# Hand-placed buffers in one memory tile, late weights over attention buffers, and a mixture token part spread over head pairs

## The chip, the core and the metric

The kernel runs on one core of a Trainium2 chip. A core has five engines that run side by side and meet at semaphores: TensorE (PE in the profile, with PEld for its weight loads), VectorE (DVE), ScalarE (ACT), GpSimd (POOL) and SyncE (SP). Matrix products go to a small memory of eight banks, PSUM; everything else is worked on in the larger SBUF; DMA engines carry data between the chip's main memory and SBUF. The metric is device time in microseconds, the median of the runs shown, lower being better.

## The reference

Attention comes first, then a soft mixture of experts over its result. There are 8 batches, 12 heads, 448 tokens and a head width of 64. The mixture sees the 3584 tokens with 768 features each, and has 8 experts with 4 slots each and a hidden width of 1024.

```
scores = (q @ k^T) / sqrt(64);  m = max over keys;  e = exp(scores - m)
attn   = e / (sum(e) + exp(-m) + 1e-9);   x = (attn @ v) as [3584 tokens, 768]
logits = x @ phi                                  # [3584, 32 slots]
d = softmax of logits over the tokens;  slot_input = d^T @ x
slot_out[e] = relu(slot_input[e] @ w1[e]) @ w2[e] # eight experts, four slots each
c = softmax of logits over the slots;   out = c @ slot_out
```

All inputs are 32-bit floats. The kernel works on 16-bit floats (bf16), which its transfers write directly. The eight experts' weights are 50 MB in main memory; the kernel handles them as 32 pieces of 768 KB in bf16 (expert, matrix, half). Queries, keys and values together are 33 MB in main memory.

## The kernel before, in words

**A fast path and a fallback.** The kernel holds two complete programs. The fast path leaves out the maximum m, since exp(scores) without it divides to the same result as long as no sum overflows. It keeps every denominator in `den_all`, and at its end it counts on how many of the 112 partitions all denominators are below a limit: `fine` compares (L495), `good` takes the minimum per partition (L496), and a matrix product of `good` with a column of ones gives the count, which is cast to a whole number in `n_good` (L498, L499). Each engine then loads that number and branches (L593, L594): if it is below 112, the whole of `general_path` (L23 to L172) runs behind the fast path and computes everything again, with maxima, one head at a time and 112 query rows at a time.

**`general_path`.** Its attention is 8 x 12 x 4 = 384 blocks of 112 query rows. Each block makes one score product (L56), a maximum on DVE (L58) and its scaling (L59), an exponential with its sum on ACT (L62), a second exponential of the maximum (L64), two sums and a reciprocal on DVE (L65 to L67), four transposes of the exponentials on PE (L70), their copy on DVE (L72), four products with the values (L75) and a division on DVE (L77). Per head there are two more copies (L52). The transposes and the output have one PSUM buffer each, the scores two. Behind it come 32 blocks of token logits (L88 to L97), a softmax over all tokens, 32 blocks of slot inputs (L106 to L112), the experts one after the other with one buffer for each weight matrix (L124 to L148), and 32 blocks of output with one output buffer (L151 to L172). A scheduler sets its instructions' order, under a queue per engine.

**The fast path's attention.** It is written under a manual schedule: each engine's queue is in the order of the text. The 96 heads are taken as 48 pairs, six to a batch; the loop of L468 runs over pairs `g`, and inside it over four parts `c`. In one round the pair `g` gets its scores (`scores`, L319) and its exponentials on ACT (L321), the pair `g-1` is multiplied with its values and divided (`attend`, L332 to L342), and the pair `g+1` is transposed (`transposes`, L309, copied by DVE at L314). POOL copies the pair `g+2` out of the staging buffers (`arrange`, L299 to L301) and also issues all loads (`load_in`, L250; `load_weight`, L229). The values have four buffers `va`, the exponentials two. A wait in POOL's queue therefore holds up every load behind it.

**The mixture's token part.** `moe_pieces(b-1)` is a list of nine pieces for a finished batch: three transposes of its tokens (L357, L360), two halves of the logits (L373) with the running softmax over tokens, transposes of the softmax weights, two slot-input products (L430), and a transpose of the slot softmax. One piece is run in each of the last two parts of a round, from the second pair of the next batch on.

**Weights and tail.** Staging takes six buffers of the size of a weight piece, two sets of three, each holding a whole batch. Weight pieces go to seventeen buffers of their own; three are issued with each batch. After the last round six pieces go to the staging buffers, and the remaining nine to a new pool, `late`, whose memory was that of the attention (L510 to L513). The experts run in two rounds of four (L536 to L570); each round needs both matrices of its four experts. The output is formed in eight pieces of 1344 KB (L578 to L591).

Of the kernel before, what the change touches and what calls it, by code (L numbers as in the profile page):

```python
# [19 lines left out]
DEN_LIMIT = float(2.0 ** 60)  # L20
# [155 lines left out]
def kernel(  # L176
# [23 lines left out]
    NG = B * HP  # L200
    scale = 1.0 / (D ** 0.5)
    SP_ = 464
    ND = DD // 2

    cst = ctx.enter_context(tc.tile_pool(name="cst", bufs=1))

    with ExitStack() as fast:
        fast.enter_context(tc.manual_schedule())


        units = fast.enter_context(tc.tile_pool(name="units", bufs=1))
        UW = H * T * D

        def unit(i, shape, name):
            u = units.tile([128, UW], BF16, tag=f"u{i}", name=name)
            return u

        NU = 23
        free_units = list(range(6, NU))
        wt = {}  # L220

        def load_weight(e, m, half, u):
            if m == 0:
                dst = u.rearrange("p (j f) -> p j f", j=KC)
                src = moe_w1[e].rearrange("(j p) f -> p j f", p=128)[:, :, ts(half, F // 2)]
            else:
                dst = u.rearrange("p (k d) -> p k d", d=DD)
                src = moe_w2[e].rearrange("(k p) d -> p k d", p=128)[:, ts(half, FK // 2), :]
            nc.gpsimd.dma_start(out=dst, in_=src)  # L229
            wt[e, m, half] = dst  # L230

        weight_order = [(e, m, h) for e in range(E) for m in range(2) for h in range(2)]


        qn, kn, va = {}, {}, {}
        ident = cst.tile([128, 128], BF16, name="ident")
        acc = cst.tile([NS, DD], F32, name="acc")
        dsum = cst.tile([NS, 1], F32, name="dsum")
        ones = cst.tile([128, 1], BF16, name="ones")
        n_good = cst.tile([1, 1], I32, name="n_good")  # L240
        cT_all = cst.tile([128, B, 128], BF16, name="cT")

        heads_src = lambda a, b, h0, h1: a[b, h0:h1].rearrange("h (p t) d -> p h (t d)", t=T)

        def load_in(b, parts):
            st = [unit(3 * (b % 2) + i, None, f"in{3 * (b % 2) + i}") for i in range(3)]
            for h0, h1 in parts:
                for a, u in zip((k, q, v), st):
                    vw = u.rearrange("p (h x) -> p h x", h=H)
                    nc.gpsimd.dma_start(out=vw[:KT, h0:h1, :], in_=heads_src(a, b, h0, h1))  # L250
            kn[b], qn[b], vn[b] = [u.rearrange("p (h t d) -> p h t d", h=H, t=T) for u in st]

        vn = {}
        load_in(0, [(0, 2), (2, H)])
        make_identity(nc, ident)
        nc.vector.memset(acc, 0.0)
        nc.vector.memset(cT_all, 0.0)
        nc.vector.memset(dsum, 0.0)
        nc.vector.memset(ones, 1.0)

        with ExitStack() as at:
            ent = at.enter_context
            abuf = ent(tc.tile_pool(name="abuf", bufs=1))
            va_buf = [abuf.tile([128, 2, T, D + 1], BF16, name=f"va{i}") for i in range(4)]
            eT_buf = [abuf.tile([128, T, 2, SP_], BF16, name=f"eT{i}") for i in range(2)]
            for i in range(4):
                nc.gpsimd.memset(va_buf[i][:, :, :, D:], 1.0)
            for i in range(2):
                nc.vector.memset(eT_buf[i][:, :, :, S:], 0.0)
            phi_sb = abuf.tile([128, KC, 4, NS], BF16, name="phi")  # L270
            phi_f = abuf.tile([128, KC, NS], F32, name="phif")
            Z = abuf.tile([128, S], BF16, name="Z")
            den_all = abuf.tile([128, NG * 2 * T], F32, name="den")
            nc.sync.dma_start(out=phi_f, in_=moe_phi.rearrange("(j p) s -> p j s", p=128))
            nc.vector.memset(Z, 0.0)
            for r in range(4):
                nc.vector.tensor_copy(phi_sb[:, :, r, :], phi_f)
            p_in = ent(tc.tile_pool(name="p_in", bufs=3))
            p_qk = ent(tc.tile_pool(name="p_qk", bufs=2))
            p_x = ent(tc.tile_pool(name="p_x", bufs=2))  # L280
            p_xT = ent(tc.tile_pool(name="p_xT", bufs=1))
            p_w = ent(tc.tile_pool(name="p_w", bufs=2))
            ps_S = ent(tc.tile_pool(name="ps_S", bufs=2, space=PSUM))
            ps_t = ent(tc.tile_pool(name="ps_t", bufs=1, space=PSUM))
            ps_o = ent(tc.tile_pool(name="ps_o", bufs=2, space=PSUM))
            ps_m = ent(tc.tile_pool(name="ps_m", bufs=1, space=PSUM))

            qk, tp, xb, ob = {}, {}, {}, {}

            k2, q2, va = {}, {}, {}  # L290

            def arrange(g):

                b, hp = divmod(g, HP)
                hs_ = slice(2 * hp, 2 * hp + 2)
                k2[g] = p_in.tile([128, T, 2, D], BF16, name="k2")
                q2[g] = p_in.tile([128, T, 2, D], BF16, name="q2")
# [5 lines left out]
            def transposes(g, c):  # L303
                b, hp = divmod(g, HP)
                if c == 0:
                    tp[g] = ps_t.tile([128, 2 * S], BF16, name="tp")
# [42 lines left out]
            def moe_pieces(b):  # L349
# [18 lines left out]
                def logits(i):  # L368
                    def f():
# [5 lines left out]
                        if i == 0:  # L375
                            return
# [249 lines left out]
```

## Time and profile before

| what | value |
| --- | --- |
| median of three runs (range) | 338.07 us (337.82 to 339.64) |
| time of the profiled execution | 338.76 us |
| its span, first to last instruction | 337.0 us |
| first and last exponential of the attention (L321) | 10.07 and 236.06 us |
| late weights: first issued, last landed | 253.9 and 292.1 us |
| first product of the output (L583) | 297.34 us |
| DMA traffic | 53.3 MB moved, of which 11.0 MB is output |

The span is measured inside one profiled execution, and the time of that execution is 1.76 us longer than its span; it lies 0.2% above the median. The rows of the groups list read as: line, engine, operation, output and inputs with their shapes and count, then the busy time and mean duration of one, then the idle time of that engine just ahead of these instructions and who ended it. In the slices of the span each digit is a tenth of a slice's time.

### The profile page before, as it was taken

The numbers are of one execution on the slowest core, as the hardware profiler recorded it, in microseconds if no ns is written. First come the engines' busy times: TensorE is split into PE (matmuls) and PEld (weight loads), VectorE is DVE, ScalarE is ACT, GpSimd is POOL, SyncE is SP. The second block draws the span as 40 slices with busy tenths as digits, with TensorE's granted clock in tenths as the row PEclk, the third lists the DMA queues.
The fourth block names the chain that finished last, engine by engine and source line by source line (L and its number), as shares of the span: only waits on it lengthen the run. The fifth ranks groups of instructions, "written<-read, shape, count | busy, mean of one in ns | idle before, by whom it ended". The sixth has DMA issues, their size and how long they took to land.

```text
span 337.0 us, 7264 instructions
## 1 busy us (share of the span) xinstructions
PE 234.8 (70%) x2963; PEld 133.8 (40%) x2963; DVE 167.0 (50%) x497; ACT 194.4 (58%) x245; POOL 134.3 (40%) x223
## 2 busy tenths in 40 slices
PE   0439999799799899979989978988640565641210
PEld 0125566456456446545645645644310122310000
DVE  3104456657567656675665757667451020153440
ACT  1237898689789769879867978988020000033330
POOL 8195494294377438439427443460007300000000
PEclk9999999789999969999978999999755595775555
DMA  7999999989959949979947900069927999539994
GB/s 95 162 123 202 202 159 205 169 108 203 208 71 199 209 70 191 205 129 157 204 77 90 160 2 0 2 95 210 208 52 113 208 211 207 107 113 341 343 342 179
DMA packets 55530, 53.34 MB, mean 158 GB/s; under 512 B 1856, under 2 KB 54592, under 8 KB 54592
## 3 DMA queue, kind: packets, MB, share of 16 engines
q0 software_dynamic: 53680, 41.68, 81.2%
q1 hardware_dynamic: 1808, 11.11, 9.4%
q8 instruction: 25, 0.41, 0.5%
q14 instruction: 17, 0.14, 0.1%
HBM read 83.46 MB, written 11.01 MB: 280 GB/s over the span
## 4 chain that ended last, share of the span: by engine, by line
PE 34%; DMA 20%; ACT 20%; DVE 15%; issue 6%; POOL 2%; ACTq 0%; DVEq 0%; SPq 0%; POOLq 0%
ACT eT L321 16%; DMA late<-in_moe_w_dram 11%; PE o L332 11%; PE s L319 9%; DMA out_dram<-ot 6%; PE m L430 4%; PE m L373 3%; PE tp L309 3%; DMA in<-in_q_dram 3%; DVE xT L360 3%; DVE x L342 2%; DVE qk L314 2%; DVE ot L587 2%; ACT Z L388 2%; PE m L357 2%
## 5 line engine op out<-in xcount | busy, mean ns | idle before, releaser
L321 ACT ACTIVATE eT<-s 112x896 bf16<-112x896 f32 x192 | 166.6, 915 | 43.8 <-PE s L319 41.4
L332 PE MATMUL o<-va,eT 112*128 112x65 bf16 x1536 | 89.8, 201 | 4.9 <-ACT eT L321 4.5
L332 PEld LDWEIGHTS <-eT 112*128 112x128 bf16 x1536 | 62.9, 101 | 49.1 <-issue 41.2
L319 PE MATMUL s<-qk 64*128 64x448 bf16 x384 | 74.4, 383 | 6.8 <-ACT eT L321 5.3
L301 POOL COPY va<-in 112x512 bf16<-112x512 bf16 x48 | 29.9, 623 | 94.5 <-PE o L332 92.3
L339 DVE TENSOR_SCALAR den<-o 112x4 f32<-112x4 f32 x96 | 15.3, 159 | 60.9 <-PE o L332 59.2
L342 DVE TENSOR_TENSOR x<-o,rd 112x256 bf16<-112x256 f32 x96 | 40.7, 424 | 3.3
L309 PE MATMUL tp<-ident,k 112*128 112x112 bf16 x192 | 32.1, 223 | 13.4 <-POOL k L299 13.4
L314 DVE COPY qk<-tp 128x896 bf16<-128x896 bf16 x48 | 29.4, 612 | 11.0 <-PE tp L309 11.0
L309 PE MATMUL tp<-ident,q 112*128 112x112 bf16 x192 | 32.0, 225 | 3.2 <-POOL q L300 3.2
L319 PEld LDWEIGHTS <-qk 64*128 64x128 bf16 x384 | 20.9, 94 | 33.1 <-issue 19.3
L299 POOL COPY k<-in 112x512 bf16<-112x512 bf16 x48 | 30.0, 624 | 2.5 <-DMA in<-in_k_dram 2.5
L300 POOL COPY q<-in 112x512 bf16<-112x512 bf16 x48 | 29.9, 622 | 2.3 <-DMA in<-in_q_dram 2.3
L309 PEld LDWEIGHTS <-k 112*128 112x128 bf16 x192 | 18.2, 102 | 14.4 <-POOL k L299 14.0
L587 DVE COPY ot<-f 112x1536 f32<-112x1536 f32 x8 | 14.1, 1757 | 17.1 <-DMA out_dram<-ot 15.4
L589 ACT COPY ot<-f 112x1536 f32<-112x1536 f32 x8 | 11.5, 1438 | 18.9 <-DMA out_dram<-ot 17.7
L583 PE MATMUL f<-sor,cT 32*128 32x384 bf16 x64 | 6.7, 470 | 21.2 <-ACT ot L589 20.3
L309 PEld LDWEIGHTS <-q 112*128 112x128 bf16 x192 | 19.6, 102 | 3.7 <-POOL q L300 3.7
L430 PE MATMUL m<-x,dz 112*128 112x384 bf16 x64 | 18.1, 422 | 1.8 <-DVE acc L436 1.1
L229 POOL DMA_DIRECT2D late<-in_moe_w_dram x9 | 7.2, 833 | 30.1 <-DVE rs L524 28.2
L341 DVE RECIPROCAL rd<-den 112x4 f32<-112x4 f32 x96 | 17.1, 178 | 3.3
L229 POOL DMA_DIRECT2D in<-in_moe_w_dram x23 | 18.3, 819 | 0.0
(80 smaller groups left out, 205.6 us busy)
## 6 DMA issues: line engine op xcount, KB each, us to landing
in<-in_moe_w_dram POOLq DMA_DIRECT2D x23, 768.0 KB, 18.5
out_dram<-ot SPq DMA_DIRECT2D x8, 1344.0 KB, 6.1
late<-in_moe_w_dram POOLq DMA_DIRECT2D x9, 768.0 KB, 19.9
in<-in_k_dram POOLq DMA_DIRECT2D x7, 672.0 KB, 7.3
in<-in_q_dram POOLq DMA_DIRECT2D x7, 672.0 KB, 10.4
in<-in_v_dram POOLq DMA_DIRECT2D x7, 672.0 KB, 12.8
in<-in_k_dram POOLq DMA_DIRECT2D x1, 560.0 KB, 7.5
in<-in_q_dram POOLq DMA_DIRECT2D x1, 560.0 KB, 9.5
```

The source lines that it names most:

```text
L229: nc.gpsimd.dma_start(out=dst, in_=src)
L299: nc.gpsimd.tensor_copy(k2[g][:KT].rearrange("p t h d -> p h t d"), kn[b][:KT, hs_])
L300: nc.gpsimd.tensor_copy(q2[g][:KT].rearrange("p t h d -> p h t d"), qn[b][:KT, hs_])
L301: nc.gpsimd.tensor_copy(va[g][:KT, :, :, :D], vn[b][:KT, hs_])
L309: nc.tensor.transpose(tp[g][:, ds(i * S + t * KT, KT)], n[:KT, t].rearrange("p h d -> p (h d)"), ident[:KT, :KT])
L314: nc.vector.tensor_copy(qk[g], tp[g])
L319: nc.tensor.matmul(s[:, h, :S], qk[g][ds(h * D, D), ds(c * KT, 128)], qk[g][ds(h * D, D), ds(S, S)], start=True, stop=True)
L321: nc.scalar.activation(eT_buf[g % 2][:KT, c, :, :S], s[:KT, :, :S], AF.Exp, scale=scale)
L332: nc.tensor.matmul(o[:, t, :], eT_buf[g % 2][:KT, j, h, ds(t * KT, 128)], va[g][:KT, h, j, :], start=(j == 0), stop=(j == T - 1))
L342: nc.vector.tensor_mul(xb[b][:KT, :, ds((2 * hp + h) * D, D)], o[:KT, :, :D], rd[:KT].unsqueeze(2).to_broadcast([KT, T, D]))
L430: nc.tensor.matmul(m, lg[2][:KT, t, :], xb[b][:KT, t, ts(half, ND)], start=(t == 0), stop=(t == T - 1))
L587: nc.vector.tensor_copy(o[:KT, :, ts(half, ND)], f[:KT, :, :ND])
```

## The change

The fast path is written anew around one tile `mem` of 106,072 bf16 elements per partition, from which `take` hands out places one behind the other; `general_path` is as it was.

- **Weights.** The order is now all 16 pieces of the first matrix, then the 16 of the second. Piece `i` goes to `unit[i]`. Units 0 to 21 are their own; 22 to 24 also hold the staging; 25 to 31 are laid over the attention's buffers. The last two pieces are each loaded in two halves.
- **Staging.** `load_in` loads half a batch (three pairs); a stage is three places of 1536 elements.
- **Denominators.** A row of the value buffer under an extra contraction row carries 1 + 1e-9, so that the sum comes out of the product; `rd_all` holds the reciprocals, and the limit is on these. Value buffers: three.
- **Token part.** Each round transposes the tokens of pair `g-2` and adds one product to the logits; the softmax over tokens, the slot inputs and the slot softmax follow in the last parts of later rounds. Transposes of all kinds share the one PSUM buffer `ps_t`.
- **Experts.** Both rounds of four experts add up in one PSUM tile: their slots are laid into 32-column groups with zeros elsewhere. The selection product is gone.
- **Check.** `fine` is now written over `xT` and `good` over the first column of `Z`. `good` is written before the experts; the last `load_weight` is issued between the two halves of the first matrix, and the product that counts `good` stands behind both halves.
- **Output.** Sixteen pieces of 672 KB out of four buffers.

```diff
-DEN_LIMIT = float(2.0 ** 60)
+RDEN_LIMIT = float(2.0 ** -60)
...
+        mem = ent(tc.tile_pool(name="mem", bufs=1)).tile([128, 106072], BF16, name="mem")
...
+        unit = [take(UW) for _ in range(NW + 3)]
+        late = top[0]
+        xbuf0 = take(T * DD)
+        kq = [[take(T * 2 * D) for _ in range(2)] for _ in range(2)]
...
+        xbuf1 = take(T * DD)
+        va2 = take(va_w)
+        xT = take(S)
+        Z = take(S)
...
+        NL = (top[0] - late) // UW
+        unit += [mem[:, late + i * UW:late + (i + 1) * UW] for i in range(NL)]
...
+        st = [[u[:, i * 1536:(i + 1) * 1536] for u, i in s_] for s_ in
+              (((unit[NW], 0), (unit[NW], 1), (unit[NW + 1], 0)),
+               ((unit[NW + 2], 0), (unit[NW + 2], 1), (unit[NW + 1], 1)))]
...
+            if i + 2 < len(w_order):
+                nc.gpsimd.dma_start(out=dst, in_=src)
+            else:
+                for n in range(2):
+                    nc.gpsimd.dma_start(out=dst[:, ts(n, 2), :], in_=src[:, ts(n, 2), :])
...
-                    nc.vector.tensor_scalar(dn, o[:KT, :, D], 1e-9, 1.0, ALU.add, ALU.add)
-                    rd = p_w.tile([128, T], F32, name="rd")
-                    nc.vector.reciprocal(rd[:KT], dn)
+                    rd = rd_all[:KT, ds((g * 2 + h) * T, T)]
+                    nc.vector.reciprocal(rd, o[:KT, :, D])
...
                 if g + 2 < NG:
+                    arrange_kq(g + 2, nc.gpsimd)
+                if g + 1 < NG:
+                    arrange_v(g + 1)
+                if o == 1 and (i + 2) * GP < NG:
+                    load_in(i + 2, [(0, 2 * GP)])
+                if (o == 2 or (o == 0 and i % 2)) and w_next[0] < NW:
+                    load_weight()
+                if g == NG - 6 or g == NG - 3:
+                    load_weight()
+                    if g == NG - 3:
+                        load_weight()
...
+                    if c == 2 and g >= 2:
+                        x_transposes(g - 2)
+                    if c == 3:
+                        if g >= 2:
+                            logits(g - 2)
...
+            for _ in range(NL - 1):
+                load_weight()
...
+        fine, good = xT[:, :NG * 2 * T], Z[:, :1]
+        nc.vector.tensor_scalar(fine[:KT], rd_all[:KT], RDEN_LIMIT, None, ALU.is_gt)
+        nc.vector.tensor_reduce(good[:KT], fine[:KT], axis=AX.X, op=ALU.min)
...
+            for half in range(2):
+                if half:
+                    c_transposes(B - 1)
+                    load_weight()
+                for r in range(R):
+                    for j in range(KC):
+                        for g in range(G):
+                            nc.tensor.matmul(hp_[ds(32 * g, 32), half, :], siT[:, j, r, g, :],
...
+            nc.tensor.matmul(mg[:1, :1], good[:KT], ones[:KT], start=True, stop=True)
+            nc.vector.tensor_copy(n_good, mg[:1, :1])
...
     fine_parts = nc.values_load(n_good, min_val=0, max_val=KT)
     with tc.If(fine_parts < KT):
         general_path(nc, tc, ident, q, k, v, moe_phi, moe_w1, moe_w2, out)
```

## The prediction

> **What bounds the kernel now.** I read the page first (busy shares, slices, chain), then the waits, then the chain in order of time from the end of the attention on, then ACT's timeline, and at last the groups with shapes, for prices.
>
> ```profile
> span 337.0 us, 7264 instructions
> PE 234.8 (70%) x2963; PEld 133.8 (40%) x2963; DVE 167.0 (50%) x497; ACT 194.4 (58%) x245; POOL 134.3 (40%) x223
> ...
> PEclk9999999789999969999978999999755595775555
> ...
> GB/s 95 162 123 202 202 159 205 169 108 203 208 71 199 209 70 191 205 129 157 204 77 90 160 2 0 2 95 210 208 52 113 208 211 207 107 113 341 343 342 179
> ```
>
> No engine is full over the span: it has stages. Slices 1 to 28 are the attention, with transfers that pause (the slices of 71, 70 and 77 GB/s); then a stretch with almost no traffic (2, 0, 2), a second run of weights at about 210, and the output at about 342 GB/s.
>
> ```profile
> 96.33 4.24 ACT L321 ACTIVATE eT<-s 112x896 bf16<-112x896 f32 x5 [0.58 <-PE s L319]
> ...
> ACT eT L321 <- PE s L319: 41.4, 53, 8.1
> ...
> POOL late L229 <- DVE rs L524: 28.2, 1, 28.2
> ...
> 253.91 8.03 DMA late<-in_moe_w_dram
> ...
> 262.23 29.91 DMA late<-in_moe_w_dram
> ```
>
> Back to back, an exponential takes 4.24 / 5 = 0.85 us, so 192 take 163 us; they are spread over 226 us (10.07 to 236.06). The waits say why: ACT stood 41 us for scores, in PE's queue behind the bunched mixture pieces and a late first load. POOL then stood 28 us on the last reciprocal of the fast attention before the nine late weights could start: 38.2 us of transfers, 4.25 each, with nothing else on the chain.
>
> **The change part by part: the fast path.** (L579, L587, L378 and L538 are lines of the changed kernel, the others of the one before.) The sum goes along the path that sets the end.
>
> Attention. The exponentials stay 192 x 0.85 = 163. ACT keeps per batch 0.62 + 0.19 + 0.28 + 0.31 = 1.4 us of mixture work by its rows, about 1.1 in issue spacing: 9 in all (the cast of `Z`, 0.52, goes to DVE). From a first exponential at 10 the floor is 182; with every old bubble kept it is 236. A pair's extra PE work is now about one product and four transposes instead of two pieces at once, but x, softmax and slot transposes share one PSUM buffer with the pair's own, so PE still waits for DVE's copies. I take 0.4 us of bubble per pair, 19 in all, near the better end because the work that made the old bubbles is spread: last exponential at 200. DVE loses 96 x 0.159 = 15 (denominators), gains about 8 x 0.5 (cast) and 48 x 0.37 - 24 x 0.613 = 3; it was half idle. POOL gains 24 loads x 0.90 = 22 us and stays under its idle 94 us in front of L301. Its three instead of four value buffers let it run one pair less ahead; that is covered by its 3.6-us pair against 1.9 of copies.
> Transfers in this time: 25 of 32 weights (25 x 3.75 at 210 GB/s = 94) and the inputs (24 x 672 KB, about 3.3 each, 79): 173 of 190 us. That is a narrow cover.
>
> Behind the attention: the old kernel needed 236.06 to 255.05 (19.0). Three rounds of x transposes (3.2) and most of six logits products are gone, leaving about 14: slot inputs transposed at 214.
>
> Late weights. Unit 25 waits only for batch 6's slot inputs, so six transfers start near 196; the last needs the slot softmax (about 219) but queues behind them: 7 x 4.25 = 29.8, landed at 227. The old wait of 28 is gone; what is late next is the experts' second matrix. One wait is new: on PE, the count (L579) stands ahead of the transposes of L587, and it must wait for half of the last weight (below). So the whole second matrix comes behind all transfers: transposes 1.0, two copies 1.4, 128 products at 2.79 / 64, 5.6, copy 0.6: 8.6. Selection products (1.3) are gone.
>
> Output. 11.0 MB at 342 GB/s = 32.2, a first product and copy 2.0, last landing 2.1: 36. End of the fast path: 227 + 9 + 36 = 272, with 250 to 300 as its bounds.
>
> **The change part by part: the count and the branch.** `Z` begins at `late` + 19,416 elements (the sum of what `take` gave before it). Unit 31 covers 18,432 to 21,504. Its first half, up to 19,968, therefore holds `good`, at offset 984: the second row of that half, column 216. In program order `good` is written (L538), then this half is loaded over it, then L579 multiplies `good` with ones. In the built program that product's weight load waits for exactly this transfer's semaphore. So it does not count partitions: it adds 112 weights of expert 7 (rows 640 to 751 of `w2`, column 216), 0.07 in the reference's draw. Cast to a whole number that is 0, below 112, and `general_path` runs behind the fast path. (Likewise the last pair's values are copied out of unit 23 after a weight was loaded there; that copy waits for the transfer about two pairs before it is needed, and costs nothing.)
>
> The trace never ran `general_path`, so it is priced from rows of the same or near shapes.
>
> ```profile
> L381 DVE TENSOR_REDUCE nm<-m 32x1 f32<-32x448 f32 x8 | 4.9, 612 | 2.9 <-PE m L373 2.5
> ...
> L407 DVE COPY dz<-m 112x512 bf16<-112x512 bf16 x8 | 3.3, 416 | 0.3 <-PE m L405 0.3
> ...
> L385 DVE TENSOR_TENSOR nmx<-nm,nmx 32x1 f32<-32x1 f32 x7 | 1.0, 148 | 0.2
> ...
> L388 ACT ACTIVATE Z<-m,nmx 32x448 bf16<-32x448 f32 x8 | 5.0, 624 | 0.2
> ...
> L394 ACT ACTIVATE al<-nmx 32x1 f32<-32x1 f32 x7 | 1.9, 277 | 0.0
> ...
> L446 DVE COPY cT<-m 128x112 bf16<-128x112 bf16 x8 | 1.7, 208 | 0.3 <-PE m L444 0.3
> ...
> L434 DVE COPY acc<-m 32x384 f32<-32x384 f32 x2 | 1.1, 546 | 1.4 <-PE m L430 1.4
> ...
> L583 PE MATMUL f<-sor,cT 32*128 32x384 bf16 x64 | 6.7, 470 | 21.2 <-ACT ot L589 20.3
> ```
>
> The width decides these, not the partitions. One of the 384 attention blocks on DVE: maximum 0.61; four operations on a column, 0.15 each; copy of 448 columns 0.37; division of 64 columns 0.18; and two copies of 0.37 per four blocks, 0.19. With about 0.03 between dependent ones that is 2.2 us. Round the engines (queue to queue), from one scaled maximum to the next: exponential and its sum 0.81 (0.62 + 0.19), four transposes 0.57 at half clock (four at L405 took 0.68 there and 0.43 at full clock), copy 0.37, two column operations 0.30, hand-overs 5 x 0.05: 2.3. Queues in order cost a little more where both meet: I take 2.35, 384 x 2.35 = 902. From below: DVE's bare busy time, 1.94 x 384 = 745. From above: no overlap at all, scores 0.55, maximum 0.61, scale 0.15, exponential 0.81, transposes 0.68, copy 0.37, products 0.45, division 0.18, hand-overs 0.4: 4.2 x 384 = 1610. Two buffers nearly everywhere put it near the lower end.
>
> The row that decides on PE's pace is the granted clock:
>
> ```profile
> 250.00:270.00 20.00, 6.63 (x60) 2.41 (x58) 2.88 (x9) 0.60 (x1) 8.98 (x19) 0.50 0.84 140
> 270.00:290.00 20.00, 12.12 (x154) 5.20 (x150) 3.32 (x5) 1.08 (x2) 0.00 (x0) 0.71 1.19 209
> 290.00:310.00 20.00, 7.84 (x90) 2.93 (x83) 6.29 (x5) 5.27 (x5) 0.00 (x0) 0.63 0.50 168
> ```
>
> These are stretches of the tail (the first column is the stretch, then its length, then busy time of PE, PEld, DVE, ACT and POOL, then the granted clock). PE a third busy was granted 0.50, at 39% 0.63, at 61% 0.71. A block keeps PE busy 0.57 + 0.45 + 0.55 of 2.35 us, 67%, so the clock lies between half and full, and the price at half clock is the careful one. [...]
>
> Behind the attention, in order: 32 blocks of logits, six transposes and six products each, about 1.05 on PE: 34. Softmax over 3584 columns by the rate of L381 and L388: 3.9 + 3.7 = 8. Slot inputs, 32 x 0.85 (two products of 384 columns 0.32 each, one transpose): 27; with scaling and transposes 7. Experts: both weights are loaded as whole matrices, 8.5 each by the late weights' 4.25 per half, and one buffer each: products of the first 6.6 (12 x 0.43 and two activations), eight transposes and copies 4, second 6.3 (16 x 0.32 and two copies): 17 per expert, about the 10.4 of a load plus one matrix; 8 x 16.5 + 10 = 142. Output: one buffer, so each block waits for its predecessor's landing: two divisions 1.1, a product 0.5, hand-overs 0.3, a transfer of 344 KB about 3.0 (between 2.2 for 96 KB and 6.1 for 1344): 4.95 x 32 = 158, and a cast 4. Sum 34 + 8 + 27 + 7 + 142 + 162 = 380; bounds 280 (full clock, 2.5 per output block) and 520.
>
> Sum: 272 + 902 + 380 = 1554; with the 1.8 us outside the span 1556. The profiled execution lies 0.7 us above the median, which does not matter here.
>
> **The rivals.**
> 1. The branch is not taken. That needs the count to read `good` before the weight lands, or its column to lie elsewhere; then the kernel is the fast path alone, 272 + 1.8, about 274 and faster. For it: the rewritten path is the shorter one by every stage above. Against it: the offsets, and a wait that fixes the order. It decides at one point, whether the number in `n_good` is 112.
> 2. The fallback runs nearly serially. If the single buffers of transposes and output let DVE and PE take turns, a block takes 3.4 us or more: 272 + 384 x 3.4 + 380 = 1958. For it: one buffer each for `g_pt` and `g_o`, in-order queues. Against it: DVE has the next block's maximum to do in that time.
> 3. The fallback is bound by DVE alone at full PE clock, with prefetched weights: 272 + 745 + 280 = 1297.
>
> [...]
>
> **How the numbers follow.** The fallback near my price 0.78, serial 0.12, DVE-bound 0.05, not taken 0.05. The predicted time is 1556. The range reaches from 1340 (between rival 3 and the sum) to 1900 (3.25 us per block), and leaves out rival 1, the far part of rival 2 and most of rival 3, about 0.2. Faster by over 0.5% 0.05, slower 0.95; 0.5% is about what a measurement of this kernel can tell.
>
> **What would show it.** In the profile after: instructions at lines 45 to 172, over 20,000 more, and a span of over 1300 us. L587 waits on PE for the last weight's transfer; the last exponential of L378 near 200 and the first output near 238. In the fallback DVE above 80% busy, blocks of about 2.35 us. If `n_good` is 112, no line below 175 appears and the whole forecast fails; if the block is mis-sized, only its term does.

## The result, and the profile after

The changed kernel takes 1487.38 us (median of four runs, 1484.30 to 1488.67) against 338.65 for the kernel before in the same comparison: 4.39 times as long, interval 4.375 to 4.406. The forecast was 1556 with a range of 1340 to 1900. The direction and its cause were right; the sum was 69 us high, and its terms were further off than that, in opposite directions. Some executions are disturbed, slower at a lower granted clock (0.824 to 0.830 in the first experiment, where the others had 0.873 to 0.884); the ratios are of the undisturbed ones alone, and so is the time of 344 us in the first experiment (343.14, 344.21 and 345.39; the other three took 352.36 to 353.64).

The page of the changed kernel, the lines that answer to those shown of before:

```profile
span 1485.3 us, 23575 instructions
...
PE 1144.3 (77%) x8101; PEld 702.9 (47%) x8101; DVE 903.7 (61%) x3695; ACT 549.6 (37%) x1493; POOL 313.1 (21%) x538
...
PEclk9899998675555555555555555555558556675555
...
GB/s 157 164 126 150 153 149 104 129 225 107 23 22 25 21 23 25 23 22 23 24 21 23 25 24 21 23 25 21 23 6 1 24 188 171 175 122 74 75 75 74
```

A slice is now 37 us. The first nine or so are the fast path, at 104 to 225 GB/s. Then come nineteen slices of 21 to 25 GB/s and a clock of 5 tenths: the fallback's attention. The rest is its logits, slot inputs, experts (171 to 188 GB/s) and output (74 to 75). The lines of `general_path`, never seen in the trace of before, lead the groups. A row gives the median duration of one between its extremes, and the first and the last start in us:

```profile
L62 ACT ACTIVATE g_e<-g_sc,g_nm x384: 622/633/634, 352.6 to 1105.0; 112x448 bf16<-112x448 f32 x192
...
L77 DVE TENSOR_SCALAR gx<-g_o,g_den x384: 264/282/286, 355.7 to 1108.0; 112x64 bf16<-112x64 f32 x192
```

From here the span can be cut into three parts without remainder: 352.6 up to the fallback's first exponential, 755.4 for its 384 blocks (1.97 each), and 1485.3 - 1108.0 = 377.3 behind them.

The end of the fast path, in the timeline:

```profile
279.73 0.80 PE L452 MATMUL t<-mem 112*128 112x384 bf16 x2 [15.10 <-DMA mem<-in_moe_w_dram]
...
286.59 0.71 POOL L296 DMA_DIRECT2D mem<-in_moe_w_dram  x1 [23.91 <-DVE mem L542]
...
295.94 0.17 PE L579 MATMUL t<-ones,mem 112*1 112x1 bf16 x1
...
296.20 0.15 DVE L580 CAST n_good<-t 1x1 int32<-1x1 f32 x1 [2.36 <-PE f L570]
...
298.36 8.74 PE L593 MATMUL f<-mem 128*32 128x384 bf16 x128 [0.32 <-DVE mem L589]
```

POOL issues the load of the last weight's first half at 286.59. The last to use its place before that is L538, which writes `good` there at 285.38 (the profile names L542, a later step of DVE that works elsewhere). The count at 295.94 reads the column `good` in that place 9.35 us after the issue; the half weight has landed by 291, from when on nothing moves until 295. And one line was not foreseen: PE stands 15.10 us in front of the last batch's slot inputs (L452), and what it waits for is a weight.

The attention's own waits (engine, line, what was waited for: us in total, times, longest; up to 300 us):

```profile
ACT mem L378 <- PE s L376: 52.9, 72, 5.8
...
PE t L405 <- DVE mem L370: 16.8, 39, 0.6
...
PE t L452 <- DMA mem<-in_moe_w_dram: 16.1, 2, 15.1
...
PE l L420 <- DVE mem L408: 9.2, 9, 1.6
```

ACT waited 41.4 us for scores in the kernel before; here it is 52.9. The rewritten attention did not get shorter: its exponentials run from 15.7 to 258.4, 243 us, where they had taken 226.

### The profile page after: what moved, and what is told of

The parts are those of the page before. It is cut to its first block, busy times and chain, and to the rows that moved or that the text cites. A ratio compares the mean times of both kernels' runs of the same rounds, so it can differ in the third digit from the quotient of the medians.

```text
span 1485.3 us, 23575 instructions
## 1 busy us (share of the span) xinstructions
PE 1144.3 (77%) x8101; PEld 702.9 (47%) x8101; DVE 903.7 (61%) x3695; ACT 549.6 (37%) x1493; POOL 313.1 (21%) x538
## 5 line engine op out<-in xcount | busy, mean ns | idle before, releaser
L62 ACT ACTIVATE g_e<-g_sc,g_nm 112x448 bf16<-112x448 f32 x384 | 243.1, 633 | 443.1 <-PE g_sc L56 233.9
L70 PE MATMUL g_pt<-ident,g_e 112*112 112x112 bf16 x1536 | 237.2, 309 | 46.0 <-ACT g_e L62 46.0
L58 DVE TENSOR_REDUCE g_nm<-g_sc 112x1 f32<-112x448 f32 x384 | 238.6, 622 | 17.1 <-PE g_sc L56 0.6
L56 PE MATMUL g_sc<-g_nT,g_nT 64*112 64x448 bf16 x384 | 237.2, 619 | 0.5 <-DVE g_nT L52 0.5
L75 PEld LDWEIGHTS <-g_eT 112*112 112x112 bf16 x1536 | 179.6, 199 | 107.1 <-DVE g_den L66 39.4
L75 PE MATMUL g_o<-g_n,g_eT 112*112 112x64 bf16 x1536 | 215.4, 281 | 13.4 <-DVE g_den L66 1.0
L70 PEld LDWEIGHTS <-g_e 112*112 112x112 bf16 x1536 | 176.8, 205 | 60.2 <-ACT g_e L62 59.3
L72 DVE COPY g_eT<-g_pt 112x448 bf16<-112x448 bf16 x384 | 150.2, 391 | 84.8 <-PE g_pt L70 58.2
L378 ACT ACTIVATE mem<-s 112x896 bf16<-112x896 f32 x192 | 170.1, 913 | 57.3 <-PE s L376 52.9
L50 PE MATMUL g_tp<-ident,g_n 112*64 112x112 bf16 x768 | 110.8, 301 | 12.4 <-DMA g_n<-in_q_dram 12.1
L50 PEld LDWEIGHTS <-g_n 112*64 112x64 bf16 x768 | 70.5, 158 | 85.2 <-issue 84.9
L140 DVE COPY g_hT<-g_htp 128x4 bf16<-128x4 bf16 x64 | 10.2, 160 | 132.8 <-PE g_htp L139 132.8
```

The lines of the kernel that those rows point to most:

```text
L50: nc.tensor.transpose(p[:, ts(t, KT)], n[i][:, t, :], ident[:KT, :KT])
L56: nc.tensor.matmul(sc, nT[0][:, ts(t, KT)], nT[1], start=True, stop=True)
L58: nc.vector.tensor_reduce(nm, sc, axis=AX.X, op=ALU.max, negate=True)
L62: nc.scalar.activation(e, sc, AF.Exp, bias=nm, scale=scale, accum_out=den)
L70: nc.tensor.transpose(pt[:, j, :], e[:, ts(j, KT)], ident[:KT, :KT])
L72: nc.vector.tensor_copy(eT, pt)
```

## The experiments

**Does the column `good` decide the branch?** The first run gives it a tile of its own and changes nothing else.

```diff
+    good_col = cst.tile([128, 1], BF16, name="good")
...
-        fine, good = xT[:, :NG * 2 * T], Z[:, :1]
+        fine, good = xT[:, :NG * 2 * T], good_col
```

> The column `good` gets a tile of its own; nothing else moves, so the count's product still stands behind the first matrix of the experts. With the branch not taken the output comes from the fast path alone, in which the last batch's slot inputs and the last pair's values are read from places that already hold weights. Theory (the count read a weight and called the fallback): the count is 112, no line below 175 runs, and the time is the fast path as the profile of the changed kernel shows it, last copy ended at 338.2, landing about 2.7 later, with 1.8 outside the span: 343 us. My forecast of the fast path alone: 274. If something else took the branch: 1487 again.

Measured: 1.0116 times the kernel before (interval 1.0036 to 1.0195), about 344 us. One column, two bytes on each partition, is therefore worth about 1143 us, and nothing else of the change starts the fallback. The same run refutes the forecast's term for the fast path: it takes 344 alone, not 274. Its output is wrong: the last pair's values and the last batch's tokens are still read from places that already hold weights. In the changed kernel the fallback writes over that, so what the branch costs also pays for the right result.

**What does the second overlay cost?** Besides the load over `good`, two loads are issued ahead of the last reader of their place: one over the last pair's values (unit 23), one over the last batch's tokens (unit 30). The second run, on top of the first, puts both behind it; the load of unit 24 moves along with the first.

```diff
-                if g == NG - 6 or g == NG - 3:
+                if g == NG - 6:
                     assert w_next[0] >= NW
                     load_weight()
-                    if g == NG - 3:
-                        load_weight()
+                if g == NG - 2:
+                    load_weight()
+                    load_weight()
...
-            for _ in range(NL - 1):
+            for _ in range(NL - 2):
                 load_weight()
             z_transposes()
             slot_in(B - 1, 0)
             slot_in(B - 1, 1)
+            load_weight()
```

> As the run before, and two loads are put behind the readers of their places: the load over the last batch's tokens behind the slot-input products, and the load over the last pair's values one pair later. Theory (PE's slot inputs stood 15.1 + 1.0 us on a transfer into the tokens' place): the experts start 16 us earlier, the late transfers then just keep up, and the time falls from 343 to about 327. Rival (the transfers set the end of the experts anyway): no change, 343.

Measured: 333.49 us (331.45 to 334.71), 0.981 of before (0.975 to 0.987). The wait is gone; in its timeline the slot inputs follow at once:

```profile
263.09 1.08 PE L453 MATMUL t<-mem 112*128 112x384 bf16 x4 [0.39 <-DVE mem L447]
```

So the 15.1 us were the program's order and not a transfer that came late: a load written ahead of the last reader of its place makes the reader wait for the load, and hands it the weight; with both loads moved the output is right. It was worth about 11 us of the end (344 to 333.5), and the expected 327 was 6 too low. Why not the whole 16 is open: late weights do not take the rest, since in the profiled execution the first product of the output starts at 289.1, where it was 307.7, and PE waits for no weight on the way.

**Is the fallback's price its own?** The kernel before, with the number of good partitions set to zero behind the count.

```diff
             nc.vector.tensor_copy(n_good, m[:1, :1])
+            nc.vector.memset(n_good, 0)
```

> The kernel before, with the number of good partitions set to 0 behind its count, so that its own fast path is followed by the fallback. Theory (the fallback is added to whatever stands ahead of it, and costs 1485.3 - 341 = 1144): 338 + 1144 = 1482 us. Rival (the changed memory or queues of the changed kernel made the fallback dearer or cheaper): more than 20 us from that.

Measured in one run: 1469.06, within 20 us of the 1482 expected. The kernel before took 339.85 beside it, so the branch costs it 1469.06 - 339.85 = 1129 us. Its fallback has nearly the same pace, 384 blocks in 330.6 to 1093.1, 1.99 us each against 1.97.

```profile
L62 ACT ACTIVATE g_e<-g_sc,g_nm x384: 623/633/634, 330.6 to 1090.1; 112x448 bf16<-112x448 f32 x192
```

Both kernels are within 20 us of each other once both take the branch: 1469 and 1487. The whole factor of 4.39 is the branch, and the rest of the change costs about 1%, as the first run showed.

**Where did the fast path's gain go?** Three runs on top of the second. The first puts the x transposes into the unused half of the attention output's PSUM bank, so that they no longer share `ps_t` with the pair's own transposes.

```diff
-                    ob[h] = ps_o.tile([128, T, D + 1], F32, name="o")
+                    bank = ps_o.tile([128, 512], F32, name="o")
+                    ob[h] = bank[:, :T * (D + 1)].rearrange("p (t d) -> p t d", t=T)
+                    xo[0] = bank[:, 288:512].bitcast(BF16)
...
-                m = ps_t.tile([128, S], BF16, name="t")
+                m = xo[0] if g < NG - 2 else ps_t.tile([128, S], BF16, name="t")
```

> The kernel with the loads behind their readers (333 us), and the token transposes of a pair go to the unused half of the PSUM bank of its attention output instead of the one buffer that all transposes share. Theory (the shared buffer makes PE wait for DVE's copy, 17.2 us of waits at the token transposes, and each wait opens a gap in the exponentials): a pair without mixture softmax falls from 4.18 to about 3.8 us, the whole by 15 to 20, to about 316. Rival (DVE's copies are late anyway and PE waits for them at the logits product instead): no change, 333.

Measured: 315.81, 0.930 of before (0.919 to 0.941). As expected to 0.2 us, but not quite by the expected way. The wait at the token transposes (17.2 us in 40 pieces in the run before it) is gone, and of the 10.2 at the logits 0.8 is left. In their place PE now waits at the products with the values (L393), in whose bank the tokens lie until DVE has copied them. Two rows of the page:

```profile
L379 ACT ACTIVATE mem<-s 112x896 bf16<-112x896 f32 x192 | 167.2, 912 | 41.9 <-PE s L377 40.0
...
L393 PE MATMUL o<-mem 112*128 112x65 bf16 (+1 forms) x1536 | 86.8, 201 | 19.8 <-DVE mem L411 19.6
```

PE's waits for DVE's copies thus fall only from 27.4 to 20.4 us, and yet ACT's wait for scores falls from 50.6 to 40.0. The order of the waits in PE's queue must matter, and no run takes that apart.

The second moves the second half of the softmax over the slots out of the part `c == 2`, behind the slot inputs. There DVE, waiting for ACT in it, no longer holds up the copy of the tokens that PE's logits product needs.

```diff
-                    if c == 2 and hp == 3 and 2 * HP - 3 <= g < NG:
-                        c_softmax(1)
...
                             elif hp == 3:
                                 slot_in(b - 1, 0)
+                                c_softmax(1)
```

> The kernel with the loads behind their readers (333 us), and the second half of the slot softmax goes behind the logits and the slot inputs of its round. Theory (DVE waits in it for ACT and holds the copy of the tokens, PE stands 1.6 us at the logits product and runs at half clock behind that; seven times): 1.6 + 1 to 2 each, 18 to 25 us less, about 312. Rival (only the wait goes, not the slow clock): 11 us less, 322; if the half softmax holds the next round's copies instead: no change.

Measured: 320.62, 0.947 of before (0.936 to 0.957): the rival's 322, not the theory's 312. Only the wait itself goes (10.2 us at the logits before, 0.8 now). No clock is gained: the mean granted one is 0.877, where it was 0.879.

The third has both, and a smaller fill of the exponentials' buffers ahead of the first pair.

```diff
-            nc.vector.memset(a.rearrange("p c h s -> p (c h s)"), 1.0)
+            nc.vector.memset(a[96:128].rearrange("p c h s -> p (c h s)"), 1.0)
+            nc.vector.memset(a[:, :, :, S:], 1.0)
```

> Both edits together, and the two buffers of exponentials are filled with ones only where the last 32 partitions or the padding columns need it, instead of whole (two fills of 3.15 us ahead of the first copy). Theory: the first exponential comes 5 us earlier (15.6 to about 10), and with 15 to 20 and 18 to 25 from the other two the time is about 333 - 42 = 291. If transfers bound the attention (176 us of them at full rate ahead of its end): about 305.

Measured: 304.86, 0.901 of before (0.893 to 0.909). It beats both kernels, by 10% and by a factor of 4.9. It is the number of the rival that had the transfers as the next bound, but that is no proof of it. The gains of the two runs alone add up to 333.49 - 17.68 - 12.87 = 302.9 without any new bound. A line of its page (queue, packets, MB, share) and two of its waits:

```profile
q0 software_dynamic: 54096, 41.69, 91.7%
```

```profile
ACT mem L380 <- PE s L378: 26.4, 42, 6.2
...
PE t L369 <- DVE mem L317: 13.3, 1, 13.3
```

The load queue's share is 91.7%, where it was 81.2% before, but it moves the same 41.7 MB in a span that is shorter by a tenth, and no engine waits for an input or a weight for longer than 0.6 us during the attention. And the smaller fill gained nothing: PE still stands 13.3 us ahead of its first transposes (12.7 before), since a fill of 32 partitions takes 3.15 us, as long as one of 128. So no run tests what a shorter fill would be worth.

**What holds the clock at one half?** The forecast had to choose between half and full clock for the fallback. Half was right, but its reason was not: PE is not idle. In the windows (stretch, length, busy time of PE, PEld, DVE, ACT, POOL, granted clock, DMA share, GB/s) of the changed kernel:

```profile
700.00:900.00 200.00, 185.08 (x1120) 126.82 (x1119) 166.55 (x762) 85.59 (x305) 39.69 (x77) 0.50 0.20 23
...
1108.00:1112.00 4.00, 3.64 (x35) 2.99 (x35) 1.95 (x6) 0.00 (x0) 0.00 (x0) 0.50 0.00 0
1112.00:1120.00 8.00, 6.88 (x101) 5.43 (x99) 5.93 (x17) 0.00 (x0) 0.00 (x0) 1.00 0.01 2
```

PE is busy 93% of the attention at 0.50, and the logits reach 1.00 within 4 us of their start. Six variants with idle work for PE, added to the changed kernel and run once each, ask what the difference is. All added products go to a spare PSUM bank that nothing reads. First three more products per block, with 64 rows contracted (as the scores have) and then with 112:

```diff
                         for j in range(T):
                             nc.tensor.transpose(pt[:, j, :], e[:, ts(j, KT)], ident[:KT, :KT])
+                        wm = psw.tile([KT, S], F32, name="g_wm")
+                        for _ in range(3):
+                            nc.tensor.matmul(wm, nT[0][:, ts(t, KT)], nT[1], start=True, stop=True)
```

> The changed kernel with three more score products (448 columns each, into a PSUM bank that nothing reads) in every block of the fallback. If the granted clock follows how much of the time the array really streams columns: it rises from 0.50 towards 1, the extra 0.56 us per block at full clock are paid by faster own products, and the time stays within 60 us of 1487. If the clock stays at 0.50 in this loop whatever PE does: 1.12 us more per block, 384 x 1.12 = 430, about 1910 us.

```diff
+                        for _ in range(3):
+                            nc.tensor.matmul(wm, ident[:KT, :KT], e, start=True, stop=True)
```

> The changed kernel with its fallback, and in each of its blocks three more products of 448 columns that contract 112 rows into 112 columns, where those of the earlier run with more products contracted 64 rows; nothing reads them. If the granted clock follows the share of the array at work: it rises above 0.50, and the time stays well under 1875. If not: 1875 us again, clock 0.50.

Measured: 1875.13 and 1867.67, near what was expected if the clock stays (1910 and 1875). Windows of the one with 64 rows, then of the one with 112:

```profile
800.00:1000.00 200.00, 193.49 (x942) 115.05 (x941) 111.12 (x506) 55.20 (x202) 26.27 (x51) 0.50 0.13 15
```

```profile
900.00:1100.00 200.00, 192.85 (x949) 110.72 (x947) 114.59 (x508) 56.47 (x204) 26.21 (x51) 0.51 0.13 15
```

Busier, and no faster. So neither the busy share nor a few products with more rows is the cause. (It also shows that PE sets the pace of the blocks: three products of 0.37 us more make a block 1.01 us longer.) Next the length of the unbroken stretch: 40 products of 64 rows in front of each batch (against the changed kernel), and 12 instead of 3 products of 112 rows in each block (against the run just shown).

```diff
+                    if h == 0:
+                        wm = psw.tile([KT, S], F32, name="g_wm")
+                        for _ in range(40):
+                            nc.tensor.matmul(wm, nT[0][:, :KT], nT[1], start=True, stop=True)
```

> The changed kernel with 40 unbroken products of 448 columns (64 rows contracted, into a PSUM bank of their own) put in front of the scores of the first head of each of the eight batches of the fallback; they add work and change no result. In the fallback's logits the granted clock went from 0.50 to 1.00 at about 1112 us, some 3.5 us after products without a pause had begun. Theory (a stretch of that length without a pause raises the clock, and the pauses of the blocks lose it again): the clock rises inside each burst, a burst takes about 9.5 us (10 products at 0.37, 30 at 0.19), the stretch of blocks behind it is back at 0.50 after a few us, and the time is 1487 + 8 x 9.5 = 1563. Rival 1 (the clock, once raised, holds through blocks whose only interruptions are copies by DVE): blocks run at 1.00 from the first burst on, DVE bounds them at about 1.8 us, and the time is about 1487 + 76 - 65 = 1498. Rival 2 (something else holds the clock down in this loop, and a burst does not help): bursts take 40 x 0.37 = 15 us each, 1487 + 119 = 1606.

```diff
-                        for _ in range(3):
+                        for _ in range(12):
                             nc.tensor.matmul(wm, ident[:KT, :KT], e, start=True, stop=True)
```

> The changed kernel with 12 products more per block of the fallback's attention (112 rows contracted, 448 columns, into a PSUM bank of their own), where an earlier run had 3; they add work and change no result. At half clock they last 12 x 0.37 = 4.5 us without a pause. Theory (a stretch of about 3.5 us without a pause raises the clock): the granted clock in the attention goes well above 0.5, to between 0.7 and 1.0, and a block takes between 3.3 (all at full clock) and 5 us: 2000 to 2650 in all. Rival (a pause anywhere in a block is enough to keep it down, or something else does): 0.50, a block takes about 4.5 + 1.8 = 6.3 us, and the time is about 1487 + 384 x 4.3 = 3140.

Measured: 1616.75, which is rival 2's 1606 and not the theory's 1563, and 2495.07, inside the theory's 2000 to 2650 and far from the rival's 3140. The two seem to contradict each other, until one looks at the rows. The burst, in the timeline of the first:

```profile
354.93 15.09 PE L58 MATMUL g_wm<-g_nT,g_nT 64*112 64x448 bf16 x40 [0.47 <-DVE g_nT L53]
```

Fifteen microseconds without a pause, at a granted clock of 0.50 to the end. It is the only one of the eight bursts that stayed together: the scheduler dealt the products of the other seven out between the blocks' own, over 22 us each. The last two runs repeat each with the rows exchanged: the burst with 112 rows (70 products of 256 columns), the blocks with 64.

```diff
-                        wm = psw.tile([KT, S], F32, name="g_wm")
-                        for _ in range(40):
-                            nc.tensor.matmul(wm, nT[0][:, :KT], nT[1], start=True, stop=True)
+                        wm = psw.tile([KT, T * D], F32, name="g_wm")
+                        nv = n[0].rearrange("p t d -> p (t d)")
+                        for _ in range(70):
+                            nc.tensor.matmul(wm, ident[:KT, :KT], nv, start=True, stop=True)
```

> As the run with 40 products in front of each batch of the fallback, which lasted 15.09 us without a pause at a granted clock of 0.50, but with 70 products of 256 columns that contract 112 rows instead of 64 (15 us at half clock). Theory now (it is the rows: a stretch of some 3.5 us raises the clock only if its products use most of the array's rows): the clock goes to 1.00 inside each burst, a burst lasts about 3.5 + 54 x 0.11 = 9.4 us, and the time is about 1487 + 8 x 10.5 = 1571, the blocks behind each burst falling back to 0.50. Rival (rows do not matter; a burst in front of a head is for another reason without effect): 0.50 inside the bursts, 15 us each, and the time of that earlier run, 1617.

```diff
-                            nc.tensor.matmul(wm, ident[:KT, :KT], e, start=True, stop=True)
+                            nc.tensor.matmul(wm, nT[0][:, ts(t, KT)], nT[1], start=True, stop=True)
```

> As the run with 12 more products per block, which had a granted clock of 0.87 and took 2495 us, with one difference: the products contract 64 rows instead of 112. Theory (the rows): 0.50 through the attention, a block takes about 12 x 0.37 + 1.8 = 6.3 us, in all about 3140. Rival (only the length of the stretch matters): the clock of that run and its time, 2495.

Measured: 1581.34 (theory 1571, rival 1617) and 3233.92 (theory 3140, rival 2495). The first of these times is near the theory's by luck. The theory had the clock at 1.00 inside each of the eight bursts, and it rose in one. The added products' row, and the clock in the slices of 39 us:

```profile
L59 PE MATMUL g_wm<-g_n,ident x560: 272/421/463, 344.3 to 1096.1; 112*112 112x256 bf16 x187
```

```profile
PEclk9989997865555555555555555555556755675555
```

The shortest of them lasts 272 ns; the median lasts 421. Here, too, only the first burst stayed together. The scheduler spread each of the others (from 421 us on) over 30 us, in pieces of at most six products, 1.5 us, and the clock stayed at 0.50. Spread like that, they fill PE's pauses (it is busy for all of the 32 us from 528 on) and cost less than the rival's 15 us each. So one burst of each kind can be compared. The first burst of 112 rows, and what follows it:

```profile
344.00:348.00 4.00, 4.00 (x22) 3.48 (x21) 0.77 (x2) 0.00 (x0) 1.91 (x4) 0.50 0.96 80
348.00:350.00 2.00, 2.00 (x15) 2.00 (x14) 0.00 (x0) 0.00 (x0) 0.00 (x0) 0.69 0.00 0
350.00:354.00 4.00, 4.00 (x39) 4.00 (x38) 0.00 (x0) 0.00 (x0) 0.00 (x0) 1.00 0.02 4
355.00:358.00 3.00, 1.71 (x20) 1.05 (x20) 2.17 (x8) 1.27 (x5) 1.55 (x3) 1.00 0.34 41
358.00:360.00 2.00, 1.47 (x15) 0.90 (x16) 1.66 (x9) 0.26 (x3) 1.03 (x2) 0.87 0.46 56
360.00:364.00 4.00, 3.62 (x22) 2.43 (x22) 3.35 (x17) 1.64 (x6) 0.52 (x1) 0.50 0.10 13
```

The unbroken stretch begins at 345.23. The clock goes up in the window of 348 to 350. If it is one step from 0.50 to 1.00, the values of the windows on either side, a mean of 0.69 is 1.24 us at 0.50 and 0.76 at 1.00: by this estimate it rises at about 349.2, 4.0 us in. By the same estimate (0.87 in 358 to 360) it goes back at about 359.5, some 4.6 us after the burst's end at 354.9, although PE is busy for most of that time. And the blocks with 12 products, with 64 rows and with 112:

```profile
1000.00:1200.00 200.00, 199.20 (x709) 109.03 (x708) 63.22 (x231) 25.28 (x93) 12.32 (x24) 0.50 0.06 8
```

```profile
1000.00:1200.00 200.00, 165.09 (x1007) 110.66 (x1008) 79.20 (x327) 33.52 (x132) 16.14 (x32) 0.87 0.09 10
```

PE busy for 99.6% of the time is granted 0.50; PE busy for 83% is granted 0.87. What follows: an unbroken stretch of about 4 us raised the clock where its products contract 112 rows, and none did where they contract 64, in 15 us without a pause or with PE busy for 199 of 200 us. By this, in the fallback's block, the score product (64 rows, 0.55 of each 1.8 us) would interrupt the others every time, and three products of 112 rows would be too short a stretch; that is argued, not shown. Left open: how many rows are enough; whether columns count as well (the fallback's slot inputs, two products of 112 rows into 32 columns between short transposes, keep PE busy for 28.16 of 32 us and are granted 0.50); how much of a window they must fill (the fast path, too, has score products of 64 rows, and is granted 0.8 or more in most slices of the attention); and whether it is the rows themselves, since the products of 112 rows had the identity as their stationary operand and those of 64 rows had data.

## Why the prediction was right, and where its terms were not

**The branch, right.** The forecast placed `good` inside the last weight's first half, loaded before L579 counts. With a place of its own for that column the fallback is gone. The line "L587 waits on PE for the last weight's transfer" was not seen: L579 itself followed the second half of the first matrix (its idle time is zero); the half weight, issued at 286.59, had stopped moving by 291. The order that mattered held all the same.

**The fast path, 272 forecast, about 342 measured** (output moves at over 330 GB/s until then; the branch, whose cost the forecast put at nothing, takes until 352.6). This term failed, and rival 1's 274 with it: the changed kernel without its fallback would not have been faster but 1.2% slower. Four steps of it:

- "A first exponential at 10": 15.7. Two fills of 3.15 us were put ahead of the first pair's copies on DVE and were not counted. 6 us, as far as the timeline shows; the run that was to shorten the fills did not.
- "I take 0.4 us of bubble per pair, 19 in all, near the better end because the work that made the old bubbles is spread": (243 - 163 - 9) / 48 = 1.5, 52 us more in all. This is the largest step. The sharing of `ps_t` was seen and priced too low: in 39 rounds the x transposes wait 0.4 us for DVE's copy of the queries and keys (16.8 in all), and in the softmax rounds PE stands up to 1.6. These waits also delay the scores that ACT needs next; undoing the first alone was worth 333.5 - 315.8 = 17.7 us and the second 12.9. The better end was wishful: spread over one queue and one buffer, the work's bubble was divided here and not removed.
- The offsets were worked out for units 23, 25 and 31, and not for unit 30, which lies over the last batch's tokens. 15.1 us of wait, about 11 of the end.
- The second matrix's products, 5.6 at 2.79 per 64: 8.74, 3 us. It is not the clock, which is 1.00:

```profile
300.00:310.00 10.00, 8.93 (x103) 5.56 (x94) 1.53 (x3) 1.87 (x3) 0.00 (x0) 1.00 0.01 2
```

  The first 64 take 2.6 us, as forecast, and the last 64 take 6.1. What differs is their order. In the first, four experts' products for four groups of 32 columns follow each other and start within 11 ns, four every 0.16 us. In the last they go expert by expert, one column group after the other, and every 0.16 us one or two start. The kernel before has the first order throughout, and the price was taken from there.

**The blocks, 902 forecast, 755 measured.** "DVE 2.2" came from adding up durations: 1.94 and gaps. The rows it was priced from, of 32 partitions, held for 112: the maximum over 448 columns takes 0.624 us (0.612 at L381), the exponential 0.633 (0.624 at L388). But in the trace a short operation of one block starts before that of another block ahead of it has ended:

```profile
701.25 0.62 DVE L58 TENSOR_REDUCE g_nm<-g_sc 112x1 f32<-112x448 f32 x1
...
701.79 0.15 DVE L67 RECIPROCAL g_den<-g_den 112x1 f32<-112x1 f32 x1
701.86 0.14 DVE L65 TENSOR_TENSOR g_den<-g_den,g_em 112x1 f32<-112x1 f32 x1
```

L65 starts 0.07 us after L67, which is listed with 0.15. DVE is busy 166.55 / 200 x 1.97 = 1.64 us per block, less than even the lower bound of 1.94, so that bound was none. "The round, 2.3" failed too: it adds one block's steps, and with two buffers two blocks are under way. What sets the pace is PE at half clock (three added products lengthened the block by nearly their own time), 185.08 / 200 x 1.97 = 1.82 us busy per block, where the forecast had 1.57: it had left out the eight transposes per head at L50, about 0.29 per block (110.8 us in all).

**The clock, half.** Keeping half clock was right: 0.50 over 750 us. The reason given for it, PE's busy share of 67%, was wrong; with 93%, 97% and 99.6% it stayed at 0.50.

**Behind the attention, 380 forecast, 377 measured,** and its parts too: logits 33 (34 forecast), softmax 8 (8), slot inputs and their transposes 36 (34), experts about 150 (142), output 150 (162). An output block takes 4.63 us, as the chain shows (start, us, what):

```profile
1474.76 0.63 DVE g_y L170
...
1475.43 0.49 PE g_yp L169
1475.94 0.63 DVE g_y L170
1476.58 2.69 DMA out_dram<-g_y
1479.30 0.05 DVEq L170
...
1479.39 0.63 DVE g_y L170
```

The next block waits for the transfer of this one, as forecast; the transfer takes 2.7 and not 3.0.

**The sum.** 1554 - 1485.3 = 69 = -81 (fast path and branch) + 147 (blocks) + 3. The range held, but with the blocks as forecast the time would have been 1634, with the fast path as forecast 1407: that the sum is within 5% is luck, two errors that partly cancel. Of the other signs, the fallback's DVE was 83% busy (above 80 announced) and lines 45 to 172 ran; but its blocks took 1.97 us (2.35 announced), the last exponential of L378 came at 257.5 (200), the first output at 310 (238), and 16,311 instructions more (over 20,000).

## What to carry to other kernels

Where buffers are placed by hand, list for each place every writer and reader in the program's order, small columns and the last batch's leftovers too: a load that is written ahead of a reader of its place turns into a wait of that reader (15.1 us here) and hands it the new data, and if what it reads decides a branch, a column of two bytes decides the time. Price each queue from starts that follow each other in a trace, not from durations added up; and for PE ask what clock the loop will be granted, which here did not follow how busy PE was: it rose about 4.0 us into an unbroken burst of products of 112 rows and not in 15.09 us of those of 64. Work that is spread over a loop is not free where it shares a buffer with the loop's own: another place for it was worth 17.7 of 333.5 us here.

## What was not expected of the hardware

- The granted clock: 0.50 for 15.09 us of products of 64 rows without a pause, and at 99.6% busy over 200 us; up to 1.00 after about 4.0 us of unbroken products of 112 rows (one burst), and back about 4.6 us behind them.
- A fill by DVE of 32 partitions by 3712 columns takes 3.15 us, as long as one of 128 partitions.
- At full clock 64 products of 384 columns into 32 columns of the array took 2.6 us where four column groups take turns, and 6.1 us group by group.
- Two short operations of different blocks on DVE (L67, L65) start 0.07 us apart where they are listed with 0.15 and 0.14.
- From the fast path's last copy of output to the fallback's first exponential 14 us pass (338.2 to 352.6). POOL issues the first load at 346.5, 8.3 us after the copy's end, and PE starts on its data at 349.1, after 12.1 us of idle time. What the 8.3 us consist of was not measured.
